# One order of 1,400 steps for another, with twelve zero products fewer: chunk-selected attention and a gated MLP on one core

## The chip, the core and the metric

The kernel runs on one core of a Trainium2 chip. The core has TensorE (PE in the profile; PEld is its loading of weights), VectorE (DVE), ScalarE (ACT), GpSimd (POOL) and SyncE (SP). The metric is device microseconds of one execution. The profile is of one execution, and its times count from the first instruction.

## The reference

Attention over chunks of 32 keys (batch 4, 8 heads, 768 positions, 64 dimensions): for each query an upper bound of its scores with every chunk is made from the chunk's minimum and maximum of k, the six best causal chunks are kept, and a softmax runs over them. A gated MLP with a product over positions follows.

```python
k_min = np.min(k_chunks, axis=3); k_max = np.max(k_chunks, axis=3)
ub = np.sum(np.maximum(q * k_min, q * k_max), axis=-1)      # each query with each chunk
top_chunks = np.argsort(np.where(causal, ub, -1e9), axis=-1)[..., -6:]
attn = softmax(where(selected & causal, q @ k.T / 8, -1e9)); x = attn @ v
h = np.maximum(x @ w_in, 0.0); u, v = h[..., :512], h[..., 512:]
v_n = (v - mean(v)) / sqrt(var(v) + 1e-6)
v_s = einsum('ts,bsd->btd', w_spatial, v_n) + b_spatial[:, None]
return (u * v_s) @ w_out
```

## The kernel before

The 32 heads are worked in 16 pairs (two heads share the 128 partitions), four pairs to a batch; i below is the pair, h the head in it. Loads fetch two pairs at once. Every step has a short name in a table `acts`, and a list written out in the program, ORDER, names all of them once. A loop at the end runs through it:

```python
with tc.manual_schedule():
    for name in ORDER.split():
        acts[name]()
```

An engine runs its own steps in the order of the list, one after the other; a step of one engine waits for those of others only through its data and its buffers. So the list fixes five queues at once: those of TensorE, VectorE, ScalarE, and the issues of loads on POOL's queue and of on-chip transfers and stores on SP's. The names:

- `dz`, `id0`, `id1`, `small`, `expand`, `mlat`, `mtri`: constants. `id1` (POOL, L538) finishes the identity matrix, which the transposes and `expand` (L565) need.
- `ring0` to `ring4` (L540 to L547): zero fills of the five q buffers, 0, 2 and 3 on VectorE, 1 on ScalarE, 4 on POOL.
- `khXh` (L589): copies `expand` into the half of the key operand that stays (X 0 to 3, reused by every fourth pair).
- `lk`, `lq`, `lv` (L604, L610, L615; the first ones L619), `win`, `wsp`, `wout`, `lb`: loads of keys, queries, values and weights, issued by POOL.
- `kT` (L680), `kTb` (L689): transposes of k on TensorE. `kc` copies the result out of PSUM from pair 8 on; `kmax`, `kmin` (L704) reduce it by chunks; `kb` (L731) sets up the bounds' operand; `kop` (L738, L740) puts k into the key operand, by copy up to pair 7 and by a transfer on SP after.
- `qT` (L745), `rq` (L754, L756), `ub` (L762, L765), `top` (L775), `sel` (L801): the bounds, the six best and the selection, written beside q.
- `aT` and `ac` (L820, L823): q with its selection, transposed on TensorE and copied; from pair 8 on `aTd` (L826) does it by one transposing transfer on SP. Pair 0 does it in parts: `selA0`, `aTA00`, `acA00` and so on.
- `scihg` (L833), `exihg` (L842), `tri` (L848), `av` (L859), `rc`, `nm` (L864, L869): scores in six tiles g, their exponentials, the causal triangle, the products with the values, and the division. The quotients go to one of two buffers x16.
- `x` puts x16 transposed into xT, by TensorE (`xp`, L884) and a copy in batch 0 and for pair 15, else by a transposing transfer on SP (L878).
- `vbt`, `ubt`, `sbt`, `obt` (L957), each in parts of two products: the MLP of batch b, tile t. `va`, `ua` (ScalarE), `bs`, `vs`, `vn`, `gt` (VectorE) stand between; `gd` transposes the gated tile on SP, `oc` (L1020) copies the output, `os` stores it.
- `dm` is 42 products of zeros at the start, and `dm0`, `dm1` and so on are one such product each (L895). They write a PSUM tile that nothing reads.

The MLP of a batch runs among the scores of the next one. PLAN holds the parameters: `dum` is the number of single zero products, and each name under `flip` runs on the other one of ScalarE and VectorE than it does by default (for `oc`, `ac` and `kh` the default is ScalarE, for `kc` and `kop` of pairs 2 to 7 VectorE).

Of the kernel before, what the change touches and what calls it, by code (L numbers as in the profile page):

```python
# [390 lines left out]
PLAN = {'late': 40, 'mlp_first': 8, 'qbuf': 5, 'kbuf': 6, 'vbuf': 6, 'dum': 64, 'warm0': 5.3, 'kcp': 8, 'flip': ['ac10', 'ac41', 'ac51', 'ac60', 'ac71', 'gd34', 'kc10', 'kc12', 'kc13', 'kc9', 'kh00', 'kh11', 'kop00', 'kop40', 'kop71', 'oc01', 'oc03', 'oc13', 'oc21'], 'gp': ((3, 4), (3, 5)), 'lm': 0.2, 'lm2': 1.2, 'tm': 0.8, 'dum0': 42, 'split': 1, 'rpool': (4,), 'ract': (1,)}  # L391

ORDER = """
dz id0 dm ring3 lk010 ring2 ring1 lk000 ring0 lq010 small id1 lq000 expand lk001 kh00 kh30 kh11 lk011 kT0 kh21 mlat
dm0 kTb0 lq011 kmin0 dm1 dm2 dm3 dm4 dm5 kop01 dm6 dm7 dm8 dm9 dm10 dm11 lq001 kmax0 qTb0 kh31 qT0 dm12 lk11 dm13 dm14
dm15 dm16 kb0 dm17 dm18 dm19 rq00 dm20 rq01 dm21 dm22 dm23 dm24 dm25 dm26 kop00 dm27 dm28 dm29 dm30 lk10 kh20 kT1 ub0
kmax1 kTb1 kh01 lv0 dm31 dm32 dm33 dm34 dm35 dm36 dm37 dm38 dm39 top00 dm40 dm41 kop11 dm42 qT1 kmin1 lq10 dm43 dm44
dm45 kop10 dm46 dm47 dm48 dm49 dm50 dm51 dm52 dm53 selA0 dm54 top01 kh10 mtri aTA00 dm55 kb1 dm56 dm57 dm58 sel0 rq11
lq11 aTB0 dm59 rq10 dm60 dm61 dm62 dm63 acA00 ub1 wsp0 acB0 sc000 top10 win00 sc001 ex000 aTA01 top11 sc002 lk20 ex001
acA01 sc005 kT2 sel1 ex002 sc004 kop20 lk21 ex005 sc013 ex004 sc011 kmin2 ex013 aT10 lq20 sc003 ex011 sc010 ac10 av000  # L400
ex003 kop21 aT11 lq21 ex010 sc015 av001 sc100 kmax2 ex015 av002 ac11 lv1 sc012 rc00 kb2 ex012 qT2 nm00 sc102 ex100
rq21 kT3 lk31 ex102 av010 rq20 sc014 kmax3 sc112 ex014 win21 ub2 sc101 ex112 kmin3 win11 sc104 qT3 ex101 sc111 top20
# [12 lines left out]
ex513 lq61 v01.0 bs02 av411 ex505 aT60 va04 bs00 v01.2 tri50 av412 ac60 sc514 va01 v03.0 lv3 rc41 vs02 nm41 sc603 ub7
ex603 bs01 v03.2 x4 sc511 ex514 lb top70 wsT0 ex511 av500 vs01 top71 sc512 lv4 va03 sc515 av501 sel7 wsT1 ex515 wsc0
sc600 ex512 av502 vs00 aT61 wsc1 ex600 v05.0 lq50 rc50 ac61 nm50 kT8 sc601 v05.2 kmax8 lq51 ex601 aT70 va05 sc604
kmin8 av510 lk61 ac70 sc613 sc602 u01.0 kc8 ex604 tri51 qT8 bs05 ex613 av511 wsT2 lk50 ex602 kb8 u01.2 rq80 sc611 rq81
u00.0 ex611 bs03 sc610 aT71 ua01 wsc2 av512 u00.2 ex610 vs05 bs04 sc704 wsT5 ua00 u02.0 vs04 ex704 ac71 wsT4 vs03 rc51
u02.2 rs0 nm51 sc605 sc614 wsc5 ub8 ex605 x5 ex614 sc612 wsc4 tri60 av600 ua02 sc700 vn00 av601 wsT3 ex612 vn04 sc701  # L420
ex700 u04.0 top80 av602 wsc3 sc703 u03.0 vn01 ex703 sc615 u04.2 rc60 ex701 nm60 u03.2 ua04 u05.0 top81 ua03 av610 sel8
sc702 vn03 ex615 sc710 aTd8 kT9 ex702 vn02 tri61 sc712 ex710 av611 kmin9 s00.0 lk60 ex712 u05.2 kop80 kmax9 av612
kop81 sc715 sc705 ua05 s00.2 wout1 rc61 ex715 qT9 vn05 kc9 sc711 s01.0 nm61 ex705 sc714 kop91 kb9 s00.4 rq91 tri70 x6
av700 rq90 s01.2 gt00 sc713 s02.0 ex713 gd00 av701 ub9 ex714 kT10 top90 s01.4 ex711 kop90 s02.2 top91 tri71 sc802 sel9
sc800 gt01 sc801 ex802 aTd9 av702 wout3 s02.4 ex801 rc70 wout2 s03.0 nm70 ex800 sc804 gt02 qT10 ex804 av710 kmax10
gd01 sc803 sc805 av711 sc810 ex803 s04.0 kmin10 ex805 av712 ex810 gd02 sc815 s03.2 tri80 ex815 rc71 sc812 kb10 kc10
nm71 s03.4 wout0 s04.2 ex812 x7 gt03 lv7 kT11 sc813 rq100 av800 ex813 sc811 rq101 gd03 av801 s05.0 kmax11 ex811 sc814
av802 s05.2 ex814 kop101 rc80 kmin11 s04.4 sc905 sc901 ub10 ex905 nm80 ex901 sc904 s05.4 kb11 gt04 ex904 sc900 av810
ex900 kc11 sc911 sc903 o01.0 ex911 top100 sc915 o00.0 top101 ex915 ex903 sc902 sel10 av811 o01.2 ex902 gt05 aTd10 qT11
sc910 oc01 tri90 v10.0 rq110 o00.2 tri81 kop100 rq111 sc914 v10.2 oc00 gd04 v11.0 lq60 ex914 ub11 ex910 av812 v11.2  # L430
gd05 lv5 va10 rc81 o02.0 nm81 va11 v13.0 top110 o02.2 kop110 top111 lq71 v14.0 sel11 oc02 sc912 bs10 av900 ex912 sc913
kT12 ex913 aTd11 v13.2 kmax12 v14.2 tri91 va13 av901 sc1000 kmin12 va14 sc1002 lk71 av902 ex1000 sc1012 v12.0 rc90
ex1002 nm90 o03.0 lk70 ex1012 bs11 sc1004 sc1005 av910 ex1004 bs14 qT12 av911 ex1005 o03.2 kc12 vs14 vs11 v12.2 oc03
sc1010 kop121 v15.0 va12 rq121 x8 av912 sc1003 sc1001 rc91 bs12 u10.0 ex1001 v15.2 rq120 os02 ex1010 u11.0 nm91 kop120
va15 u10.2 vs10 kop111 bs13 av1000 ua10 u11.2 os01 bs15 o04.0 ex1003 x9 kb12 kT13 ua11 vs13 tri100 o04.2 kmax13 sc1015
sc1014 oc04 sc1013 av1001 ub12 vs12 ex1014 kmin13 av1002 o05.0 ex1015 ex1013 sc1101 top120 u12.0 kc13 vs15 sc1011
rc100 top121 sc1104 ex1101 o05.2 kop130 sel12 ex1011 u13.0 nm100 os00 qT13 ex1104 kop131 tri101 u12.2 rq131 rs1 sc1100
aTd12 av1010 oc05 lv6 vn10 sc1103 sc1102 ua12 vn11 u13.2 ex1103 vn13 av1011 u14.0 ua13 vn14 u15.0 ex1100 rq130 av1012
u14.2 kb13 ex1102 rc101 vn15 u15.2 ua14 vn12 s10.0 ua15 sc1114 ub13 s10.2 top130 sc1110 sc1105 s10.4 nm101 ex1105
ex1110 s11.0 tri110 gt10 kT14 ex1114 s11.2 kmin14 lq70 gd10 s12.0 av1100 kmax14 sc1115 s11.4 ex1115 s12.2 gt11 sc1113  # L440
av1101 s12.4 kc14 gd11 sc1112 s14.0 gt12 ex1112 sc1111 av1102 top131 ex1113 s13.0 gd12 rc110 sel13 ex1111 s15.0 nm110
s14.2 tri111 sc1203 aTd13 sc1200 s14.4 ex1203 av1110 ex1200 gt14 s13.2 x10 av1111 sc1213 av1112 sc1201 ex1213 kT15
rc111 nm111 sc1202 s13.4 kmax15 ex1202 x11 sc1205 s15.2 ex1201 qT14 gt13 s15.4 ex1205 sc1215 kc15 sc1204 o10.0 ex1204
rq140 sc1210 kop151 av1200 gt15 ex1215 o10.2 os05 tri120 av1201 kb14 os03 rq141 sc1212 oc10 sc1302 kmin15 o12.0 gd13
ex1210 av1202 ex1212 ub14 rc120 sc1300 nm120 o12.2 gd15 ex1300 top140 sc1214 v21.0 ex1302 top141 v20.0 oc12 sel14
sc1310 ex1214 v21.2 sc1211 ex1310 qT15 sc1313 aTd14 ex1211 sc1303 rq150 v20.2 va21 rq151 tri121 av1210 ex1313 kb15
o11.0 gd14 ex1303 ub15 v23.0 va20 top150 av1211 sc1314 kop150 top151 sc1311 av1212 ex1314 bs20 o11.2 kop140 ex1311
# [21 lines left out]
def kernel(  # L469
# [622 lines left out]
```

## Time and profile before

| | us |
|---|---|
| median of 13 runs (201.11 to 204.09) | 202.28 |
| the profiled execution | 202.13 |
| its span, first to last instruction | 200.4 |
| TensorE busy | 191.6 |
| VectorE busy | 156.4 |
| ScalarE busy | 149.1 |
| POOL busy | 80.8 |

In groups of instructions each line has the source line, the engine and operation, what is written and read, the shapes and the count, then busy time and the mean length. In stretches of time a line gives the stretch, its length, then busy us of PE, PEld, DVE, ACT and POOL with counts, the granted TensorE clock, the busy share of the DMA queues and GB/s. In order of time a line gives start, us, engine, line and operation; in brackets stands how long the engine had been idle and what ended that. SPq is the issue of a transfer on SP. A line of DMA issues ends with the time from issue to landing. Matmuls overlap in TensorE, so that the distance between two starts, not a length, tells its rate.

### The profile page before, as it was taken

The numbers are of one execution on the slowest core, as the hardware profiler recorded it, in microseconds if no ns is written. First come the engines' busy times: TensorE is split into PE (matmuls) and PEld (weight loads), VectorE is DVE, ScalarE is ACT, GpSimd is POOL, SyncE is SP. The second block draws the span as 40 slices with busy tenths as digits, with TensorE's granted clock in tenths as the row PEclk, the third lists the DMA queues.
The fourth block names the chain that finished last, engine by engine and source line by source line (L and its number), as shares of the span: only waits on it lengthen the run. The fifth ranks groups of instructions, "written<-read, shape, count | busy, mean of one in ns | idle before, by whom it ended". The sixth has DMA issues, their size and how long they took to land.

```text
span 200.4 us, 5309 instructions
## 1 busy us (share of the span) xinstructions
PE 191.6 (96%) x2057; PEld 121.7 (61%) x2057; DVE 156.4 (78%) x475; ACT 149.1 (74%) x296; POOL 80.8 (40%) x97
## 2 busy tenths in 40 slices
PE   7989999999999999999999899999999999999992
PEld 7876778776676755565565455656555555444451
DVE  6899899999999999898798689797378337257430
ACT  5879899999989985777889873689899751664151
POOL 7999956462998143434731422011212130000000
PEclk9999999999999999999999999999999999999999
DMA  6999999999899999999999999788774265342335
GB/s 40 97 127 166 163 162 181 172 193 106 57 143 120 154 115 191 138 191 148 161 139 152 236 196 165 145 216 108 220 116 43 79 121 149 114 179 85 79 127 213
DMA packets 114761, 28.60 MB, mean 143 GB/s; under 512 B 108720, under 2 KB 111280, under 8 KB 114736
## 3 DMA queue, kind: packets, MB, share of 16 engines
q0 software_dynamic: 76544, 12.20, 88.2%
q1 hardware_dynamic: 38192, 16.06, 40.6%
q8 instruction: 16, 0.26, 0.6%
q14 instruction: 9, 0.07, 0.1%
HBM read 24.38 MB, written 6.29 MB: 153 GB/s over the span
## 4 chain that ended last, share of the span: by engine, by line
PE 67%; DMA 11%; DVE 9%; POOL 6%; ACT 2%; issue 2%; SPq 0%; POOLq 0%; DVEq 0%; ACTq 0%
PE mlp L957 39%; PE sc L833 12%; PE acc L859 8%; DMA xT<-x 5%; DMA qs<-in_q_dram 3%; DMA kh<-kT 2%; DVE kmm L704 2%; POOL k L619 2%; PE trq L745 2%; PE tra L820 1%; POOL qs L619 1%; DVE max L775 1%; DVE x L869 1%; PE ub L765 1%; PE kTp L680 1%
## 5 line engine op out<-in xcount | busy, mean ns | idle before, releaser
L842 ACT ACTIVATE e<-sc 128x512 f16<-128x512 f32 (+1 forms) x192 | 93.9, 564 | 19.3 <-PE sc L833 16.6
L833 PE MATMUL sc<-a,kh 128*128 128x512 f16 (+3 forms) x256 | 61.2, 305 | 0.7 <-DMA kh<-kT 0.4
L957 PE MATMUL mlp<-w_in_sb,xT 128*128 128x512 f16 x192 | 52.2, 379 | 0.0
L848 POOL TENSOR_SCALAR_AFFINE_SELECT e<-e 128x768 f16<-128x768 f16 x24 | 21.0, 877 | 75.6 <-ACT e L842 64.3
L859 PEld LDWEIGHTS <-e 128*128 128x128 f16 x672 | 31.3, 97 | 15.5 <-DVE x L869 1.7
L957 PE MATMUL mlp<-vn,wsT 128*128 128x512 f16 x144 | 38.8, 379 | 0.0
L859 PE MATMUL acc<-vt,e 128*128 128x65 f16 x672 | 35.8, 193 | 0.8 <-DVE x L869 0.7
L704 DVE TENSOR_REDUCE kmm<-kTp 128x24 f16<-128x768 f16 x32 | 29.6, 947 | 1.8 <-PE kTp L680 1.8
L833 PEld LDWEIGHTS <-kh 128*128 128x128 f16 x256 | 22.6, 97 | 13.4 <-DMA kh<-kT 0.9
L957 PE MATMUL mlp<-w_out_sb,gT 128*128 128x512 f16 x92 | 26.1, 379 | 0.0
L957 PEld LDWEIGHTS <-xT 128*128 128x128 f16 x192 | 17.1, 98 | 14.3 <-DMA xT<-x 0.2
L1000 DVE SCALAR_TENSOR_TENSOR g<-mlp,b_col,u 128x512 f16<-128x512 f32 x24 | 17.8, 746 | 9.0 <-PE mlp L957 6.9
L1020 ACT COPY o<-mlp 128x512 f32<-128x512 f32 x19 | 11.1, 589 | 16.9 <-PE mlp L957 16.5
L979 DVE BATCH_NORM_STATS2 stats<-vraw 128x6 f32<-128x512 f32 x24 | 15.9, 677 | 5.8 <-ACT vraw L974 5.8
L869 DVE TENSOR_TENSOR x<-acc,rec 128x384 f16<-128x384 f32 x32 | 17.6, 551 | 2.4 <-DMA xT<-x 1.9
L957 PEld LDWEIGHTS <-wsT 128*128 128x128 f16 x144 | 12.6, 97 | 10.1
L989 ACT ACTIVATE u<-mlp 128x512 f16<-128x512 f32 x24 | 14.0, 597 | 5.0 <-PE mlp L957 4.1
L775 DVE MAX8 max<-ub 128x8 f32<-128x8 f32 (+4 forms) x160 | 15.2, 163 | 1.7 <-PE ub L765 1.6
L974 ACT ACTIVATE vraw<-mlp 128x512 f32<-128x512 f32 x24 | 14.2, 608 | 2.4 <-PE mlp L957 2.4
L610 POOL DMA_DIRECT2D qs<-in_q_dram x14 | 14.5, 1045 | 1.6 <-DMA w_in_sb<-in_moe_w_in_dram 0.8
L604 POOL DMA_DIRECT2D k<-in_k_dram x14 | 14.8, 1062 | 0.4 <-DMA ws_raw<-in_moe_w_spatial_dram 0.4
L864 DVE RECIPROCAL rec<-acc 128x6 f32<-128x6 f32 x32 | 5.9, 185 | 9.7 <-PE acc L859 9.6
(85 smaller groups left out, 243.3 us busy)
## 6 DMA issues: line engine op xcount, KB each, us to landing
out_dram<-o SPq DMA_DIRECT2D x23, 256.0 KB, 2.3
vt<-in_v_dram POOLq DMA_DIRECT2D x8, 384.0 KB, 9.2
k<-in_k_dram POOLq DMA_DIRECT2D x14, 192.0 KB, 7.1
qs<-in_q_dram POOLq DMA_DIRECT2D x14, 192.0 KB, 7.0
kh<-kT SPq DMA_DIRECT2D x16, 96.0 KB, 4.9
ws_raw<-in_moe_w_spatial_dram POOLq DMA_DIRECT2D x6, 192.0 KB, 6.7
w_in_sb<-in_moe_w_in_dram POOLq DMA_DIRECT2D x8, 128.0 KB, 8.3
w_out_sb<-in_moe_w_out_dram POOLq DMA_DIRECT2D x4, 128.0 KB, 5.3
```

The lines of the kernel that those rows point to most:

```text
L604: nc.gpsimd.dma_start(out=k_tile(g)[:, :, :, hi, :].rearrange("p x t d -> p (x t) d"), in_=source(k, b, 2 * hp + 2 * hi, 2))
L610: nc.gpsimd.dma_start(out=t.rearrange("p x t d -> p (x t) d"), in_=source(q, b, 2 * hp + 2 * hi, 2))
L704: nc.vector.tensor_reduce(self.kmm[:, m, :], src, axis=AX.X, op=op, negate=(m == 1))
L775: nc.vector.max(self.max8[:, qi - 1, hi, :], self.ub[:, c0:c0 + CPT * (qi + 1)])
L833: mm(sc[:, col:col + n], lhsT=self.kh[hi][:, t * P:(t + 1) * P], rhs=self.a[:, q0 // P:(q0 + n) // P, hi, :], start=True, stop=not diag)
L842: nc.scalar.activation(out=self.e[hi][:, g * 512:g * 512 + width], in_=self.sc[hi, g][:, 0:width], func=Act.Exp, scale=scale)
L848: nc.gpsimd.affine_select(out=blk, in_=blk, compare_op=Alu.is_ge, fill=0.0, base=0, channel_multiplier=-1, pattern=[[0, NQT], [1, P]])
L859: mm(self.av[hi][:, qi, :], lhsT=self.e[hi][:, c:c + P], rhs=self.v[hi][:, t, 0:D + 1], start=first and n == 0, stop=last and n == len(blo ...
L869: nc.vector.tensor_tensor(self.x16[:, :, hi, :], in0=self.av[hi][:, :, 0:D], in1=self.rec[hi].to_broadcast([P, NQT, D]), op=Alu.mult)
L957: mm(st[kind, ti], lhsT=lhsT, rhs=rhs, start=(j == 0), stop=(j == n - 1))
L979: nc.vector.bn_stats(st["stats", ti], st["vraw"][:, ti, :])
L1000: nc.vector.scalar_tensor_tensor(g, in0=st["s", ti], scalar=b_col[:, ti:ti + 1], in1=st["u"][:, ti, :], op0=Alu.add, op1=Alu.mult)
```

## The change

The code of every step stays. PLAN and ORDER change. Single zero products go from 64 to 52. The zero fills stay on their engines (`rpool` and `ract` are as they were), but stand elsewhere in the list: `ring1` now comes after `rq01` on ScalarE, and `id1` comes after four load issues on POOL, not three. The flips put `kh00`, `kh21`, `kh30`, `kh31` on VectorE (before `kh00`, `kh11`), `ac11`, `ac40`, `ac41`, `ac51`, `ac70`, `ac71` on VectorE (before `ac10`, `ac41`, `ac51`, `ac60`, `ac71`), `kop31`, `kop40`, `kop51`, `kop71` on ScalarE (before `kop40`, `kop71`), eight `oc` on VectorE (before four), `kc8` to `kc11` on ScalarE (before 9, 10, 12, 13), and `gd34` on VectorE (before ScalarE). All five queues are in another order nearly throughout; the diff is cut to PLAN, the head, the start of the first MLP and the part around pairs 8 to 11.

```diff
-PLAN = {'late': 40, 'mlp_first': 8, 'qbuf': 5, 'kbuf': 6, 'vbuf': 6, 'dum': 64, 'warm0': 5.3, 'kcp': 8, 'flip': ['ac10', 'ac41', 'ac51', 'ac60', 'ac71', 'gd34', 'kc10', 'kc12', 'kc13', 'kc9', 'kh00', 'kh11', 'kop00', 'kop40', 'kop71', 'oc01', 'oc03', 'oc13', 'oc21'], 'gp': ((3, 4), (3, 5)), 'lm': 0.2, 'lm2': 1.2, 'tm': 0.8, 'dum0': 42, 'split': 1, 'rpool': (4,), 'ract': (1,)}
+PLAN = {'late': 40, 'mlp_first': 8, 'qbuf': 5, 'kbuf': 6, 'vbuf': 6, 'dum': 52, 'warm0': 5.3, 'kcp': 8, 'flip': ['ac11', 'ac40', 'ac41', 'ac51', 'ac70', 'ac71', 'kc10', 'kc11', 'kc8', 'kc9', 'kh00', 'kh21', 'kh30', 'kh31', 'kop00', 'kop31', 'kop40', 'kop51', 'kop71', 'oc01', 'oc03', 'oc05', 'oc11', 'oc12', 'oc13', 'oc23', 'oc25'], 'gp': ((3, 4), (3, 5)), 'lm': 0.2, 'lm2': 1.2, 'tm': 0.8, 'dum0': 42, 'split': 1, 'rpool': (4,), 'ract': (1,)}
 
 ORDER = """
-dz id0 dm ring3 lk010 ring2 ring1 lk000 ring0 lq010 small id1 lq000 expand lk001 kh00 kh30 kh11 lk011 kT0 kh21 mlat
-dm0 kTb0 lq011 kmin0 dm1 dm2 dm3 dm4 dm5 kop01 dm6 dm7 dm8 dm9 dm10 dm11 lq001 kmax0 qTb0 kh31 qT0 dm12 lk11 dm13 dm14
-dm15 dm16 kb0 dm17 dm18 dm19 rq00 dm20 rq01 dm21 dm22 dm23 dm24 dm25 dm26 kop00 dm27 dm28 dm29 dm30 lk10 kh20 kT1 ub0
-kmax1 kTb1 kh01 lv0 dm31 dm32 dm33 dm34 dm35 dm36 dm37 dm38 dm39 top00 dm40 dm41 kop11 dm42 qT1 kmin1 lq10 dm43 dm44
-dm45 kop10 dm46 dm47 dm48 dm49 dm50 dm51 dm52 dm53 selA0 dm54 top01 kh10 mtri aTA00 dm55 kb1 dm56 dm57 dm58 sel0 rq11
...
-sc410 kop71 x3 sc500 av401 ac51 v00.0 ex410 kmin7 av402 ex502 v00.2 tri41 ub6 ex500 kop70 sc504 sc503 lq41 sc505 top60
...
-ex900 kc11 sc911 sc903 o01.0 ex911 top100 sc915 o00.0 top101 ex915 ex903 sc902 sel10 av811 o01.2 ex902 gt05 aTd10 qT11
-sc910 oc01 tri90 v10.0 rq110 o00.2 tri81 kop100 rq111 sc914 v10.2 oc00 gd04 v11.0 lq60 ex914 ub11 ex910 av812 v11.2
-gd05 lv5 va10 rc81 o02.0 nm81 va11 v13.0 top110 o02.2 kop110 top111 lq71 v14.0 sel11 oc02 sc912 bs10 av900 ex912 sc913
-kT12 ex913 aTd11 v13.2 kmax12 v14.2 tri91 va13 av901 sc1000 kmin12 va14 sc1002 lk71 av902 ex1000 sc1012 v12.0 rc90
-ex1002 nm90 o03.0 lk70 ex1012 bs11 sc1004 sc1005 av910 ex1004 bs14 qT12 av911 ex1005 o03.2 kc12 vs14 vs11 v12.2 oc03
-sc1010 kop121 v15.0 va12 rq121 x8 av912 sc1003 sc1001 rc91 bs12 u10.0 ex1001 v15.2 rq120 os02 ex1010 u11.0 nm91 kop120
...
-sc1014 oc04 sc1013 av1001 ub12 vs12 ex1014 kmin13 av1002 o05.0 ex1015 ex1013 sc1101 top120 u12.0 kc13 vs15 sc1011
-rc100 top121 sc1104 ex1101 o05.2 kop130 sel12 ex1011 u13.0 nm100 os00 qT13 ex1104 kop131 tri101 u12.2 rq131 rs1 sc1100
-aTd12 av1010 oc05 lv6 vn10 sc1103 sc1102 ua12 vn11 u13.2 ex1103 vn13 av1011 u14.0 ua13 vn14 u15.0 ex1100 rq130 av1012
...
+dz id0 dm small lk010 ring0 lk000 ring3 lq000 ring2 lq010 id1 lk011 expand lk001 kh00 kT0 kh11 kh31 lq011 kh30 dm0
+kTb0 kmin0 dm1 dm2 dm3 dm4 dm5 kop01 dm6 lq001 dm7 dm8 dm9 dm10 dm11 kmax0 qTb0 mlat qT0 rq01 dm12 lk11 dm13 dm14 dm15
+dm16 rq00 dm17 dm18 dm19 dm20 dm21 dm22 dm23 kb0 ring1 kop00 ub0 lk10 dm24 dm25 top00 kTb1 kT1 top01 lv0 kop10 dm26
+dm27 dm28 selA0 dm29 kmin1 aTA00 aTA01 kh10 dm30 dm31 dm32 dm33 dm34 mtri dm35 kmax1 dm36 dm37 dm38 dm39 dm40 dm41
+kh01 dm42 dm43 dm44 dm45 dm46 dm47 lq10 sel0 qT1 acA00 kop11 dm48 kb1 aTB0 rq10 lq11 sc000 kh20 rq11 dm49 dm50 dm51
+acB0 ub1 win10 acA01 ex000 sc005 sc001 kh21 win01 ex005 top10 sc002 ex001 kT2 win21 top11 ex002 sc004 lb sc013 kmax2
+ex004 sc010 ex013 lk21 sc003 sel1 av000 kop21 ex010 sc015 aT10 ex003 lq21 kop20 aT11 ex015 sc011 ac10 av001 kmin2
+sc012 lk20 av002 ex011 sc102 rc00 ac11 ex012 sc100 kb2 ex102 nm00 qT2 wout1 qT3 ex100 rq21 sc014 lq20 sc112 rq20 ex014
...
+ex411 sc414 rq60 ex501 sc502 rq61 xp3 ex414 kmax7 sc413 ex502 av400 lk41 aT51 x2 ex413 sc500 sc410 ac51 kop71 lq40
+sc504 av401 x3 ub6 ex500 av402 kop70 v00.0 ex410 lq41 sc503 kmin7 v00.2 ex504 sc510 ex503 sc512 top60 lv3 v02.0 ex510
...
+lv7 s05.2 ex812 x7 kmax11 av801 s04.0 sc810 s05.4 rq101 ex810 kop100 sc901 kmin11 ub10 kop101 ex901 sc903 sc813 top100
+gd03 av802 ex903 o00.0 rc80 ex813 top101 sc814 s04.2 nm80 ex814 o00.2 kb11 sel10 sc911 tri81 kop111 gt05 sc904 sc914
+ex911 s04.4 aTd10 lq60 oc00 av810 gt04 sc900 ex904 av811 o01.0 ex914 lq70 sc913 ex900 qT11 o01.2 ex913 lq71 av812
+sc902 oc01 v10.0 ex902 v11.0 rc81 lv5 gd04 nm81 sc910 sc915 rq110 v10.2 ex915 rq111 sc905 o02.0 kop110 va10 lk71 v11.2
+gd05 ub11 va11 av900 lv6 top110 v13.0 ex905 o02.2 bs11 av901 v13.2 bs10 oc02 lk70 v14.0 top111 va13 kT12 vs10 sel11
+ex910 v14.2 tri90 kmin12 v12.0 va14 sc912 sc1002 kc12 v12.2 ex912 aTd11 vs11 sc1003 kmax12 av902 va12 tri91 sc1000
+o03.0 ex1002 rc90 bs14 qT12 x8 ex1000 v15.0 nm90 ex1003 o03.2 bs13 sc1010 av910 ex1010 sc1012 rq121 sc1004 rq120 u10.0
...
+oc04 sc1104 tri100 o05.0 ex1104 kc13 av1001 u12.0 ex1014 vs12 vs14 av1002 sel12 sc1011 sc1101 rc100 kmax13 sc1114
...
+sc1110 vn10 u15.2 ex1112 vn12 sc1105 u14.2 vn15 u13.0 ua14 rq131 sc1100 av1010 rq130 ua15 u13.2 vn13 ex1105 s10.0
...
 """
```

## The prediction

> **What bounds the kernel now.** I read the stages first, then who waits for whom, then the order of time at the two places where TensorE stands still. The page gives the engines' totals, and the stretches give them by stage (busy us of PE, PEld, DVE, ACT, POOL).
>
> ```profile
> span 200.4 us, 5309 instructions
> PE 191.6 (96%) x2057; PEld 121.7 (61%) x2057; DVE 156.4 (78%) x475; ACT 149.1 (74%) x296; POOL 80.8 (40%) x97
> ...
> 6.64:48.86 42.22, 39.62 (x627) 31.74 (x626) 40.89 (x136) 39.04 (x77) 31.24 (x40) 1.00 1.90 154
> 49.40:72.00 22.60, 22.60 (x287) 15.42 (x284) 22.05 (x78) 20.35 (x43) 15.12 (x15) 1.00 2.20 125
> 72.00:95.00 23.00, 22.56 (x246) 13.64 (x245) 20.95 (x59) 16.61 (x36) 10.22 (x13) 1.00 1.39 155
> 95.00:118.00 23.00, 22.23 (x235) 13.09 (x234) 18.29 (x60) 19.66 (x40) 8.99 (x9) 1.00 1.66 179
> 140.00:166.00 26.00, 26.00 (x238) 14.68 (x237) 14.16 (x33) 20.19 (x44) 5.32 (x6) 1.00 0.56 116
> ```
>
> Busy TensorE is not TensorE at its rate, so I used the distance from one matmul's start to the next: 0.216 us for 512 columns, 0.109 for 256, 0.056 for 128, 0.030 for the 65 of the value products, 0.025 for the 48 of the bounds. Summed over all real products this is 176.9 us. Of it only 32.7 us are done when the first MLP product v00.0 starts at 49.4 us: 16.7 us are lost in the head. The other 144.2 us take until 196.2 us, a loss of 2.6 us; 4.2 us of copy and store follow. So there are two bounds: up to 49 us VectorE (40.9 of 42.2 us busy) with ScalarE close behind, then TensorE, where only a late operand costs anything. The chain of waits shows such operands, all DMA landings:
>
> ```profile
> 75.40 5.00 DMA kh<-kT
> 80.45 0.82 PE sc L833 x3
> ...
> 103.85 9.26 DMA xT<-x
> 113.14 0.57 DVE x L869
> 113.75 0.45 PE acc L859 x9
> ```
>
> By the distances of starts TensorE loses 0.22 us at 76.87, 0.56 at 80.45, 0.23 at 110.02 and 0.87 at 113.75: 1.88 us.
>
> **The change, part by part.** *Zero products, 64 to 52.* They stand where TensorE waits for VectorE or a load, so twelve fewer shorten nothing by themselves: 0 us. Their other use is the clock. The 42 products of dm load their weights in 4.39 us (104 ns each), the 19 after 8 us in 1.10 us (58 ns); the granted clock is full from 6.7 us on and no gap of TensorE there exceeds 0.91 us. In the new order I find gaps up to about 1.5 us (waiting for kb0 near 9 us, for rq11 near 15 us). The Trainium skill, "TensorE: Matmul & The Clock Gate", speaks against the change here: about 3.4 us of idleness halve the clock (Part 1), and transposes don't count as busy (Part 4), and most head products are transposes. By the rule one window of 3.4 us at half speed could cost at most half of it, 1.7 us; by the row, where stretches of transposes went by at full clock, 0. I take 0, with 1.7 as upper end.
>
> *Head, VectorE.* These rows set its start:
>
> ```profile
> 3.08 0.85 POOL L619 DMA_DIRECT2D qs<-in_q_dram  x1
> 3.99 0.33 POOL L538 TENSOR_SCALAR_AFFINE_SELECT identity<-identity 128x128 f16<-128x128 f16 x1
> 4.35 0.55 DVE L565 TENSOR_SCALAR expand<-identity 64x768 f16<-64x768 f16 x1 [0.17 <-POOL identity L538]
> 4.96 1.36 DVE L589 COPY kh<-expand 64x768 f16<-64x768 f16 x2
> 6.64 1.82 DVE L704 TENSOR_REDUCE kmm<-kTp 128x24 f16<-128x768 f16 x2 [0.32 <-PE kTp L680]
> ```
>
> id1 is moved on POOL's queue behind a fourth load issue (lq010 as well as lq000): +0.85 us, and expand, which needs it, starts at 5.20. Between expand and the first kmm there are now three kh copies, not two: 1.36/2 = 0.68 more. From expand to the end of two copies took 1.97 us, so kmm starts at 5.20 + 1.97 + 0.68 = 7.85 instead of 6.64: 1.2 us late. kh21 adds a fourth copy (0.68) near 17 us. Against that, two VectorE idles go, 0.24 us (before pair 1's kmm, now behind pair 0's selection) and 0.52 (for the q of pair 2, landing at 20.27 as before): 1.2 + 0.68 - 0.76 = 1.1. The flips up to x3 cancel: kop31 and kop51 leave (2 x 0.555), ac40 and ac51 come (2 x 0.54). x3, the last copy before the first MLP, moves from 48.9 to 50.0. But 0.67 us more of TensorE's work (sc504, ub6, av402) now stands ahead of v00.0, so the TensorE-bound stretch loses 1.1 - 0.67 = 0.43.
>
> *Head, ScalarE.* ring1 (1.47 us) ran at 2.10, under the wait for expand; now it stands behind rq01, and kop10, kh10, kh01, kop11, kh20 follow it before the first exp. kop10 also needs kTb1, which TensorE now runs behind ub0 (about 10.4, so kTb1 is done near 11.5). Five copies of 0.81 bring the first exp to 15.6 instead of 14.81. ScalarE was idle for 1.1 us between there and 48.6, which takes up most of that and of the flips (two kop at 0.79 more, one ac at 0.85 less). It stays within VectorE's lag. For the head as a whole I take +0.5 us; the ends are -0.5 (both engines closer packed) and +3 (VectorE's two removed idles come back elsewhere and ScalarE's lag adds).
>
> *Copies of o.* Four more go to VectorE (0.688 each), off ScalarE (0.589), all after 84 us, where VectorE has 2 to 5 us free in each stretch above: 0. Without that room one costs 0.7 where its buffer is waited for.
>
> *The four stalls.* I measured leads: TensorE work, by the distances above, that the order puts between an issue and its first user. kop80 had 5.3 us and landed after 5.0; it now has 6.9. x8, whose landing frees the x16 buffer for pair 10, had 8.7 us to av1010 and took 9.26; it now has 13.1. The w and q loads that ran beside aTd8 come earlier. If nothing replaces them the four stalls return 1.88 us.
>
> *Loads and SP, near 90 to 115 us.* This decides. Before, POOL issued here lq60, lv5, lq71, lk71, lk70 (1152 KB in 94.55 to 102.2) and SP's transposing loads went out among them:
>
> ```profile
> 94.55 1.04 POOL L610 DMA_DIRECT2D qs<-in_q_dram  x1
> 95.58 1.44 POOL L615 DMA_DIRECT2D vt<-in_v_dram  x1
> 96.99 1.04 POOL L610 DMA_DIRECT2D qs<-in_q_dram  x1
> ...
> 100.11 2.05 POOL L604 DMA_DIRECT2D k<-in_k_dram  x2
> ...
> 98.68 3.67 SPq L826 DMA_TRANSPOSE a<-qs  x1
> ...
> a<-qs SPq DMA_TRANSPOSE x1, 11.2
> ...
> a<-qs SPq DMA_TRANSPOSE x1, 3.7
> ```
>
> The first a row is aTd11's issue, the second its time to landing, the third that of aTd13 at 125.9, when POOL had nothing in flight. aTd11 had a lead of 11.0 us and TensorE waited 0.23 us. In the new order lq70 and lv6 join the same bunch: seven issues in one piece between tri81 and tri90 (5 x 1.04 + 2 x 1.44 = 8.1 us of POOL), 1728 KB. aTd10 is issued at the first of them with a lead of 8.8 us (before 7.1; it took 5.3 in a lull), aTd11 has 8.1 to its first user sc1104, queued behind kop111, aTd10, gd04, kop110 and gd05. Behind sc1104 all of TensorE's queue stands. Bounds: aTd10 between 5.3 (lull) and 11.2 (crowd), a stall of 0 to 2.4; aTd11 between 3.7 and 11.2 x 1728/1152 = 16.8, a stall of 0 to 8.7. The two don't add up, since a stall at the first gives the second time to land. The nearest row is aTd11's own 11.2 in the lighter crowd: 3.1 at least; I take 3.5 for both.
>
> Here the rule differs from the row. "DMA: Bandwidth & Descriptors" (Queues, rings and completion order) has each DMA engine alternate between the queues with work, whatever their backlog. Two queues, equal shares: 2 x 3.7 = 7.4 us, less than 8.1, no stall. The row says 11.2 with two queues, issue time on SP included, and I follow it. lq60 (lead 10.5 for 5.9 taken), lv5 (14.0 for 9.4) and lk70 (18.1 for 15.2) still fit, narrowly. After 118 us all leads exceed the landings before (aTd13 6.0 for 3.7, gd12 4.3 for 3.2): 0.
>
> **Sum.** 200.4 + 0.5 - 1.9 + 3.5 = 202.5 us of span. The profiled execution took 202.13 us, 1.73 outside its span, and lies 0.15 under the median: 202.5 + 1.9 = **204.4 us**, 1.0% slower.
>
> **Rivals.** *The leads hold (other side).* If aTd10 lands within 8.8 us and aTd11 within 8.1, the 1.9 us return and nothing replaces them: 200.4 + 0.5 - 1.9 + 1.9 = 200.9 us. For it: seven of the eight a transfers of before landed in under 7.7 us. Against: the only one in a comparable crowd took 11.2. *The crowd scales.* The 16.8 us for aTd11 happen, 8.7 of stall instead of 3.5: 209.6; and values between. For it: DMA engines read 9 of 10 up to 125 us. Against: some bunched loads are only moved from later. *The head slips.* Its upper end, +3, without the DMA stall: 200.4 + 3 - 1.9 + 1.9 = 203.4; with half of it 205. *Nothing happens.* Searched orders trade one small stall for another: 202.3; for it, most of the work is the same products at the same rate in either order.
>
> **How the numbers follow.** Late a transfers 0.46; crowd scaling 0.14; leads hold 0.20; head slips 0.10; nothing 0.10. The first runs from 203.0 to 206.0, with a twentieth of the whole below 203.3. 0.5% of the median is 1.0 us, about what these runs can tell from none. Faster (under 201.3): most of leads-hold, 0.17. Same: the rest of it, nothing, and the lower edges of the slow cases, 0.16. Slower: 0.67. The range, 200.6 to 208.6, leaves out the best of leads-hold and the worst of crowd scaling.
>
> **What would show it.** Right: first kmm near 7.9 us, first exp near 15.6, v00.0 near 50; no wait at kop80's and x8's users; TensorE idle for some us before scores of pair 10 or 11, released by DMA a, with landings over 9 us. Wrong: those landings under 8 us; v00.0 before 49; a granted clock below 1 in the head; a new wait past 118 us.

## The result and the profile after

The changed kernel takes 205.05 us in the median (204.4 to 209.21, 11 runs), the kernel before beside it 202.66 (201.08 to 205.01, 48 runs): a ratio of 1.013, with a 95% interval of 1.0099 to 1.016. The change makes the kernel slower by about 1.3%; the forecast was 204.4 us, 1.05% slower. The profiled execution took 209.27 us, 207.6 of it span, and is one of the longest: of the 14 executions on record with their granted clock the seven at 0.996 and more took 204.4 to 205.1 us, the four at 0.988 to 0.992 took 205.8 to 206.6, and the three at 0.98, the profiled one among them, 208.6 to 209.3. Ratios, here and below, are of fast executions alone (within 1.5% of the fastest of their kernel; in e2 two of six), medians and ranges are not.

The page of the kernel after, its head and the rows of slices (each digit a fortieth of the span, tenths of busy time or of the full clock):

```profile
span 207.6 us, 5289 instructions
...
PE 192.8 (93%) x2045; PEld 121.9 (59%) x2045; DVE 159.3 (77%) x481; ACT 145.3 (70%) x290; POOL 81.0 (39%) x97
...
PE   7789989999999999999459999999999999999992
...
PEclk9999999999999999999958999999999999999998
```

TensorE has two slices at 4 and 5 tenths where everything around is at 9, and in the second of them the clock is at 5. A slice is 5.2 us, so this lies between 98.6 and 109 us. The stretches of the kernel after, with the same columns as before (length, then busy us of PE, PEld, DVE, ACT, POOL, the clock, the DMA share, GB/s):

```profile
6.64:48.86 42.22, 38.43 (x603) 30.61 (x601) 41.34 (x137) 40.12 (x78) 34.97 (x45) 1.00 1.93 160
49.40:72.00 22.60, 22.20 (x283) 15.25 (x282) 21.81 (x77) 20.09 (x42) 11.67 (x12) 1.00 1.81 114
72.00:95.00 23.00, 22.61 (x253) 14.01 (x251) 20.21 (x57) 17.90 (x37) 11.48 (x14) 1.00 1.37 155
95.00:118.00 23.00, 18.03 (x163) 10.19 (x162) 13.88 (x48) 12.25 (x26) 7.20 (x7) 0.85 1.91 151
140.00:166.00 26.00, 26.00 (x250) 14.91 (x249) 17.04 (x57) 22.02 (x48) 4.32 (x5) 1.00 0.77 164
```

The other four stretches have TensorE about as busy as before. In 95 to 118 us TensorE was idle for 5.0 us, and its records show 163 matmuls instead of 235; the DMA share rose from 1.66 to 1.91. The chain of waits of the kernel after names what ended the wait:

```profile
92.89 0.43 PE mlp L957 x2
93.33 0.06 PE sc L833
93.39 12.56 DMA a<-qs
105.95 0.04 issue
105.99 0.59 PE sc L833
106.58 0.85 PE mlp L957 x2
107.43 0.43 PE sc L833 x2
```

This is aTd10, issued at 93.39 and landed after 12.56 us; sc1002 is the first user, and all of TensorE's queue stood behind it for 5.14 us, by the distances of starts. Then comes a second loss that the chain doesn't call a wait: two MLP products of 512 columns take 0.85 us, where before and elsewhere they take 0.43. From 103.9 to 110.7 us the granted clock was one half:

```profile
103.90:110.70 6.80, 4.71 (x22) 2.32 (x22) 2.47 (x6) 2.17 (x4) 0.00 (x0) 0.50 1.64 116
```

What was around it, from the order of time of the kernel after (POOL's load issues and SP's transposing ones) and from its DMA issues between 90 and 118 us:

```profile
91.86 3.06 POOL L610 DMA_DIRECT2D qs<-in_q_dram  x3
...
93.39 2.97 SPq L826 DMA_TRANSPOSE a<-qs  x1
94.90 1.44 POOL L615 DMA_DIRECT2D vt<-in_v_dram  x1
96.29 1.05 POOL L604 DMA_DIRECT2D k<-in_k_dram  x1
97.29 1.46 POOL L615 DMA_DIRECT2D vt<-in_v_dram  x1
98.69 1.07 POOL L604 DMA_DIRECT2D k<-in_k_dram  x1
...
101.05 7.79 SPq L826 DMA_TRANSPOSE a<-qs  x1
```

```profile
vt<-in_v_dram POOLq DMA_DIRECT2D x2, 384.0 KB, 18.5
...
k<-in_k_dram POOLq DMA_DIRECT2D x2, 192.0 KB, 19.3
...
a<-qs SPq DMA_TRANSPOSE x2, 13.2
```

The seven issues of the forecast stand there in one piece, and aTd10 is issued between them. Before, a k load of this stretch landed after 15.2 us; here two take 19.3 in the median. The second row of aTd's is aTd11; it took 13.80 us and yet made TensorE wait for nothing: the wait for aTd10 had moved its user back as well.

The start of the kernel after, in order of time, for the steps of the head:

```profile
4.79 0.34 POOL L538 TENSOR_SCALAR_AFFINE_SELECT identity<-identity 128x128 f16<-128x128 f16 x1
...
5.17 0.55 DVE L565 TENSOR_SCALAR expand<-identity 64x768 f16<-64x768 f16 x1 [0.98 <-POOL identity L538]
...
5.78 1.73 DVE L589 COPY kh<-expand 64x768 f16<-64x768 f16 x3
...
7.43 1.81 DVE L704 TENSOR_REDUCE kmm<-kTp 128x24 f16<-128x768 f16 x2
```

The three copies of kh take 1.73 us together, and the first kmm starts at 7.43, not 6.64.

### The profile page after: what moved, and what is told of

Read it like the earlier page. It is cut to its first block, busy times and chain, and to the rows that moved or that the text cites. A ratio compares the mean times of both kernels' runs of the same rounds, so it can differ in the third digit from the quotient of the medians.

```text
span 207.6 us, 5289 instructions
## 1 busy us (share of the span) xinstructions
PE 192.8 (93%) x2045; PEld 121.9 (59%) x2045; DVE 159.3 (77%) x481; ACT 145.3 (70%) x290; POOL 81.0 (39%) x97
## 4 chain that ended last, share of the span: by engine, by line
PE 62%; DVE 18%; DMA 9%; POOL 6%; ACT 2%; issue 1%; POOLq 0%; DVEq 0%
PE mlp L957 40%; PE sc L833 10%; PE acc L859 7%; DMA a<-qs 6%; DVE kmm L704 4%; DMA qs<-in_q_dram 3%; DVE x L869 2%; DVE vn L994 2%; DVE max L775 2%; POOL qs L619 2%; POOL k L619 2%; PE trq L745 1%; DVE rq L756 1%; ACT e L842 1%; DVE rq L754 1%
## 5 line engine op out<-in xcount | busy, mean ns | idle before, releaser
L833 PE MATMUL sc<-a,kh 128*128 128x512 f16 (+3 forms) x256 | 62.6, 308 | 6.3 <-DMA a<-qs 5.0
L859 PEld LDWEIGHTS <-e 128*128 128x128 f16 x672 | 31.9, 98 | 14.2 <-DVE x L869 1.0
L859 PE MATMUL acc<-vt,e 128*128 128x65 f16 x672 | 36.4, 194 | 0.5 <-DVE x L869 0.4
L957 PE MATMUL mlp<-w_out_sb,gT 128*128 128x512 f16 x92 | 27.0, 385 | 0.1
L1020 ACT COPY o<-mlp 128x512 f32<-128x512 f32 x15 | 8.9, 591 | 11.6 <-PE mlp L957 11.5
L775 DVE MAX8 max<-ub 128x8 f32<-128x8 f32 (+4 forms) x160 | 15.2, 162 | 1.9 <-PE ub L765 1.8
```

What stands on the lines that cost most here:

```text
L775: nc.vector.max(self.max8[:, qi - 1, hi, :], self.ub[:, c0:c0 + CPT * (qi + 1)])
L833: mm(sc[:, col:col + n], lhsT=self.kh[hi][:, t * P:(t + 1) * P], rhs=self.a[:, q0 // P:(q0 + n) // P, hi, :], start=True, stop=not diag)
L859: mm(self.av[hi][:, qi, :], lhsT=self.e[hi][:, c:c + P], rhs=self.v[hi][:, t, 0:D + 1], start=first and n == 0, stop=last and n == len(blo ...
L957: mm(st[kind, ti], lhsT=lhsT, rhs=rhs, start=(j == 0), stop=(j == n - 1))
```

## The experiments

Theories: *crowd* says that the loss is the transposing transfers aTd10 and aTd11, late because seven loads are issued in one piece around them. *SP's queue* says that they are late behind other transfers of SP itself; e1, e4 and e9 move loads and leave SP's order as it was. *Head* says that the new start costs it (VectorE and ScalarE late). *Clock* says that TensorE's lower clock, in the head for want of zero products or behind the wait, carries part of it. Ratios are to the kernel before on the same chip, whose medians in these comparisons lay between 203.3 and 203.8 us.

| kernel | median us (range, runs) | ratio, 95% |
|---|---|---|
| e0, after itself | 206.47 (204.39 to 209.49, 6) | 1.0141 [1.0054, 1.0227] |
| e1, after, two loads later | 205.43 (203.94 to 206.37, 6) | 1.0115 [1.0051, 1.018] |
| e2, before, two loads earlier | 211.36 (207.91 to 211.57, 6) | 1.0263 [1.0155, 1.0372] |
| e3, after with the head of before | 206.88 (205.88 to 207.73, 6) | 1.0191 [1.0129, 1.0252] |
| e4, after, bunch dissolved | 205.32 (203.79 to 207.1, 10) | 1.0084 [1.0049, 1.0119] |
| e5, before with the head of after | 202.74 (201.74 to 203.49, 22) | 0.9965 [0.9944, 0.9986] |
| e6, e4 with two head steps earlier | 204.52 (203.04 to 208.4, 22) | 1.0076 [1.005, 1.0103] |
| e7, after without single zero products | 206.96 (205.82 to 209.32, 6) | 1.0149 [1.0099, 1.0199] |
| e8, after, zero products in the wait | 205.97 (205.2 to 209.22, 6) | 1.0126 [1.008, 1.0172] |
| e9, after, loads elsewhere, head as e6 | 203.22 (202.54 to 207.34, 22) | 1.000 [0.9977, 1.0024] |
| e10, e5 with two head steps earlier | 202.45 (200.93 to 204.0, 22) | 0.9962 [0.9934, 0.999] |
| e11, before itself | 203.32 (201.31 to 209.16, 22) | 0.9991 [0.9959, 1.0022] |

### e0: the changed kernel once more

No edit.

> The changed kernel itself, for a profile of a usual execution beside the others. Crowd theory (seven loads in one piece make the selection transfer of pair 10 late): 1.3% slower than the kernel before, the transfer lands over 9 us after its issue and TensorE stands 2 to 5 us before the scores of pair 10. Head theory (the later start of VectorE and ScalarE is what costs): the stall is small and the first MLP product is more than 2 us later than before.

Measured: 206.47 us, 1.0141. Its profiled execution (209.49 us) repeats the other almost to the step: aTd10 issued at 93.49, 12.86 us to its landing, TensorE stands 5.31 us ahead of sc1002, half clock from 103.93 to 110.76. So the wait comes again with the order. But this execution, too, is the longest of its six: both profiles of the changed kernel show the long kind. The link of clock and time is looser here: two executions with a clock of 0.992 took 207.25 and 208.38 us.

### e1: two of the seven loads later

```diff
-ex911 ... ex914 lq70 sc913 ...
-... va11 av900 lv6 top110 ...
+... sc1104 tri100 lq70 o05.0 ex1104 ...
+... ex1101 tri101 lv6 vs15 sc1102 ...
```

> The changed kernel with two of the seven loads, lq70 and lv6, put back behind tri100 and tri101; all else stays. Crowd theory: the transfer of pair 10 lands within 9 us, its stall falls below 1 us, that of pair 11 may keep up to 2 us: 1.5 to 3 us faster than the changed kernel. Head theory, and the theory that SP's own queue is too full: no change, within 0.5 us of the changed kernel.

Measured: 205.43 us; the profiled execution 204.65, all of it at full clock. The order of time of TensorE in e1, at the two first users:

```profile
102.06 0.38 PE L833 MATMUL sc<-a,kh 128*128 128x512 f16 x1 [1.09 <-DMA a<-qs]
...
112.36 0.38 PE L833 MATMUL sc<-a,kh 128*128 128x256 f16 x2 [1.27 <-DMA a<-qs]
```

With five loads in the bunch aTd10 lands after 8.95 us and aTd11 after 11.23; by the distances of starts the waits are 1.26 and 1.43 us instead of 5.14 and none. In the profiles the loss behind v00.0 halves, from 9.30 us in e0 to 4.57. In the times the gain over e0 is small (1.0115 against 1.0141, intervals overlapping): the median falls by 1.0 us, where 1.5 to 3 were expected. The place of two loads changes the waits, but with five the two transfers still land later than the leads allow.

### e2: the same two loads earlier in the kernel before

```diff
-v11.0 lq60 ex914 ...
+v11.0 lq60 lq70 ex914 ...
-sc1002 lk71 av902 ...
+sc1002 lk71 lv6 av902 ...
-... av1010 oc05 lv6 vn10 ...
-... kmin14 lq70 gd10 ...
+... av1010 oc05 vn10 ...
+... kmin14 gd10 ...
```

> The kernel before with lq70 moved behind lq60 and lv6 behind lk71, so that the same seven loads are in flight together; all else stays. Crowd theory: the transfer of pair 11 (11.2 us in the kernel before) takes 13 us or more and its scores wait 2 to 5 us: 2 to 5 us slower than the kernel before. Head theory and the theory of SP's queue: no change, within 0.5 us.

Measured: 211.36 us, 1.0263, the largest loss of all and larger than that of the whole change. Four of its six executions took 211.3 to 211.6 us. But the place differs from the expected one. The chain of waits of e2:

```profile
95.80 1.99 POOL qs L610 x2
97.80 13.57 DMA vt<-in_v_dram
111.36 0.14 issue
111.50 0.45 PE acc L859 x9
```

The value load lv5, issued behind lq60 and lq70, landed 13.57 us later, and av1000 waited 3.04 us for it. aTd11 took 12.18 us, less than the 13 expected, and its scores didn't wait; the kernel before reached 12.35 with five loads (e11). So moving two loads costs time without anything else of the change, but here a load came late behind other loads, not a transposing transfer. The half clock came here too, 3.41 us of it (111.79 to 115.20) behind a wait of 3.04.

### e3: the head of before in the changed kernel

```diff
-'dum': 52, 'flip': [..., 'kh00', 'kh21', 'kh30', 'kh31', 'kop00', 'kop31', ...]
+'dum': 64, 'flip': ['ac10', ..., 'kh00', 'kh11', 'kop00', ...]
-dz id0 dm small lk010 ring0 ... (after's list up to v00.0)
+dz id0 dm ring3 lk010 ring2 ... (before's list up to v00.0, for the same steps)
```

> The changed kernel with the order and the engines of the kernel before up to the first MLP product, the same steps as in its own head. Crowd theory: the first MLP product comes 0.5 to 1 us earlier and the total falls by just that, to about 0.9% over the kernel before; the stall before the scores of pair 10 stays. Head theory: the total falls by 2 us or more, to the kernel before.

Measured: 206.88 us, 1.0191. It is no faster than the changed kernel, and the gain that the head theory asks for isn't there. It says little of the head, though: v00.0 comes at 51.09 us, not earlier than the changed kernel's 50.67, so the old head's steps brought nothing forward in this order. The head is judged by e5. In its profiled execution (206.97 us) aTd10 takes 9.20 us and aTd11 12.11, with waits of 1.44 and 2.19 us, without any step of the new head.

### e4: the bunch dissolved

```diff
-... lq70 ... lq71 ... lk71 ... lv6 ... lk70 ... (between tri81 and tri90)
+av601 tri60 lq70 lq71 lk71 lk70 sc702 ...
+ex1101 tri101 lv6 vs15 ...
```

> The changed kernel with lq70, lq71, lk71 and lk70 moved forward behind tri60, where no load is in flight, and lv6 back behind tri101; of the seven loads only lq60 and lv5 stay. Crowd theory: both selection transfers land within 8 us, both stalls go (2.7 us in the profile with two loads moved), and the total falls to within 0.7% of the kernel before on either side. Theory of SP's own queue, whose order is untouched: stalls of over 1 us stay.

Measured: 205.32 us, 1.0084. aTd11 lands after 6.65 us and nobody waits for it; aTd10 still takes 9.45, and at sc1002 0.89 us are left. But the four loads now run beside the key operand of pair 8. The chain of e4:

```profile
75.98 7.60 DMA kh<-kT
83.58 0.05 issue
83.63 0.39 PE sc L833 x2
```

This wait, 1.63 us at sc803, is a new one: kop80 took 7.60 us where the changed kernel had 5.77. The loads were moved off one transfer with a short lead and onto another. This wait stands against what was won at pairs 10 and 11; only about a third of the loss came back.

### e6: e4 with two steps of the head earlier

```diff
-... lk000 ring3 lq000 ring2 lq010 id1 lk011 expand ...
+... lk000 id1 ring3 lq000 ring2 lq010 lk011 expand ...
-kh00 kT0 kh11 kh31 ...   dm23 kb0 ring1 kop00 ub0
+kh00 kT0 ring1 kh11 kh31 ...   dm23 kb0 kop00 ub0
```

> The same, and in the head id1 moved forward behind two load issues on POOL and ring1 to the front of ScalarE's queue. By my working of the head expand starts 0.9 us earlier, the first reduction 0.6 to 0.9 us earlier, the first exponential 0.5 to 1.5 us earlier, and the total falls by 0.5 to 1 us against the run without it, below the kernel before. If other waits of the head take its place, no change.

Measured: 204.52 us, 1.0076. The first kmm is at 6.85 and the first exponential at 14.51 (e4 as after: 7.43 and 15.11), and v00.0 starts at 50.01 instead of 51.09. The median falls by 0.8 us, the ratio by only 0.0008, well within the intervals. The 1.37 us at sc803 stay.

### e9: the loads at a place with room

The trace of the changed kernel shows POOL's load queue empty between the landing of lk60 at 67.3 us and the next load issue at 74.4. So four of the loads go behind lk60, and lv6 as in e1; the head is that of e6.

```diff
-kT8 lk60 aT70 ...
+kT8 lk60 lk71 lk70 lq70 lq71 aT70 ...
-... lq70 ... lq71 ... lk71 ... lv6 ... lk70 ... (between tri81 and tri90)
+ex1101 tri101 lv6 vs15 ...
```

> The changed kernel with id1 and ring1 moved as there, lv6 behind tri101, and lq70, lq71, lk71, lk70 behind lk60, so that they have landed when the selection transfer of pair 8 is issued. Crowd theory: no wait of over 0.5 us before the scores of pairs 8, 10 and 11, 1 to 1.5 us faster than with the four loads behind tri60 (ratio 1.0076): 0.999 to 1.003. If it is the number of bytes before 118 us rather than their crowding: still 1.007.

Measured: 203.22 us, 1.000 [0.9977, 1.0024]. The whole 1.3% is gone, with the same steps on the same engines, the same bytes and everything else of the new order behind the head in place. Against e6 (1.0076), which has the same head, only the place of four loads differs. The place isn't quite free: in the profile TensorE waits 0.80 us at 66.10 for a triangle of POOL that stands behind the load issues. Its profiled execution is its longest one (207.34 us): there aTd10 took 10.58 us with only lq60 and lv5 of the seven loads around it, TensorE stood 2.89 us and the clock was half for 3.41 us. So the lead at sc1002 remains short, and sometimes it still doesn't suffice. Of the 22 executions 21 took 202.5 to 204.4 us; none of these was profiled, so that the gain is shown by the times, and the waits that went by no trace.

### e5: the head of after in the kernel before

```diff
-'dum': 64, (head flips of before)
+'dum': 52, (head flips of after)
-dz id0 dm ring3 lk010 ring2 ... (before's list up to v00.0)
+dz id0 dm small lk010 ring0 ... (after's list up to v00.0, for the same steps)
```

> The kernel before with the order and the engines of the changed kernel up to the first MLP product, the same steps as in its own head. By my working x3 and the first MLP product come 1.1 us later and the total rises by 0.5 to 1.1 us. Head theory: it rises by 2 us or more. If both heads are equal: within 0.3 us.

Measured: 202.74 us, 0.9965 [0.9944, 0.9986]. The new head with 52 zero products, alone, makes the kernel no slower, by the times even 0.35% faster. Its stretches:

```profile
6.64:49.40 42.76, 39.01 (x608) 30.96 (x606) 41.92 (x138) 40.48 (x78) 31.39 (x40) 1.00 1.88 154
49.40:95.00 45.60, 45.38 (x531) 29.18 (x530) 43.79 (x136) 36.94 (x76) 24.93 (x28) 1.00 1.76 139
```

v00.0 is at 49.76, though the head steps stand where they stand in the changed kernel (first kmm 7.43, first exponential 15.10, first copy of x into xT 49.16 against 49.14). It starts before x3's copy on VectorE (50.09 us), so it doesn't need it. In the changed kernel sc504, ub6 and av402 stand ahead of v00.0 in TensorE's queue, and ub6 itself starts 0.29 us late by the distances, so that v00.0 comes at 50.67.

### e10: e5 with the two head steps of e6

Edit as in e6, on e5.

> The kernel before with the changed kernel's head, and in it id1 behind two load issues and ring1 first on ScalarE. With the head alone the ratio was 0.9965; the two moves brought the first exponential forward by 0.6 us and the first MLP product by 1.1 in the other run. Expected: first MLP product 0.5 to 1 us earlier, ratio 0.991 to 0.996, faster than both kernels. If the middle absorbs it: 0.9965 as before.

Measured: 202.45 us, 0.9962 [0.9934, 0.999]; with e5 the fastest of all, and faster than both kernels. The two moves added nothing to e5. The first exponential comes at 14.51 us, 0.6 earlier, and then TensorE's row in e10 is

```profile
18.50 0.43 PE L859 MATMUL acc<-vt,e 128*128 128x65 f16 x9 [1.18 <-DMA vt<-in_v_dram]
```

The first value load lands when it lands, so the lead won was spent waiting for it, and v00.0 is at 50.21, no earlier than e5's 49.76.

### e7: no single zero products

```diff
-'dum': 52
+'dum': 0
```

and `dm0` to `dm51` leave the list; the 42 of `dm` stay. They are all that is left out.

> The changed kernel without any of the 52 single zero products; the 42 of the start stay. By my working they shorten nothing and only hold the clock: with gaps of up to 3 us in the head the clock may fall to half for a time, and since VectorE sets the pace there, 0 to 1 us slower than the changed kernel (ratio 1.013 to 1.02). If the clock stays full: the same as the changed kernel within 0.3%.

Measured: 206.96 us, 1.0149. The stretches of e7 in the head:

```profile
4.90:10.60 5.70, 2.20 (x35) 1.80 (x36) 5.33 (x13) 3.69 (x4) 5.62 (x9) 1.00 1.63 104
10.58:17.41 6.83, 5.67 (x50) 4.54 (x51) 6.11 (x31) 5.29 (x8) 6.75 (x10) 0.50 1.90 123
```

The same stretches of the changed kernel have 4.15 us of busy TensorE in the first, and a clock of 1.00 in both. In all six executions of e7 the mean clock is 0.963 to 0.983. So the single zero products do hold the clock up in the head, and 52 of them were enough in the changed kernel's profiles. The loss of clock made v00.0 late (51.58 against 50.67), yet the times hardly show it (1.0149 against 1.0141 and 1.013): in the profiled execution the wait at sc1002 was 1.63 us instead of 5.14, with one of 1.97 us for lv5 at 113.96. That the later head shifted what follows against the loads is a guess.

### e8: zero products in the wait

```diff
-... va14 sc912 sc1002 kc12 ...
+... va14 sc912 dw sc1002 kc12 ...
+    def hold():
+        idle = ps_sc.tile([P, 512], F32, tag="sc", name="hold")
+        for _ in range(60):
+            mm(idle[:, 0:P], lhsT=idle_op, rhs=idle_op, start=True, stop=True)
```

> The changed kernel with 60 zero products (3.4 us at full clock) placed right before the scores of pair 10 that wait; their result is not read. If a wait[...] halves TensorE's clock and that is part of the loss: the clock stays full through that place, the profiled execution falls by about 2 us, the longest executions likewise, and the shortest rise by at most 1 us. If the clock is no part of it: no change or slower by up to 3 us.

Measured: 205.97 us, 1.0126. TensorE's row and the stretch that was at half clock in the changed kernel:

```profile
100.97 3.51 PE L902 MATMUL hold<-idle_op 128*128 128x128 f16 x60
104.31 0.38 PE L833 MATMUL sc<-a,kh 128*128 128x512 f16 x1
```

```profile
103.90:110.70 6.80, 6.80 (x74) 4.16 (x72) 4.02 (x11) 4.85 (x10) 0.00 (x0) 1.00 1.81 156
```

The clock stays full, and this execution took 205.32 us. It doesn't weigh the clock: aTd10 landed at 102.07 here, after 9.65 us and not 12.56, so that without the 60 products TensorE would have waited 1.1 us, too little to halve the clock by the other traces (2.19 us in e3 did not). The products (3.34 us) held TensorE 2.2 us longer than the transfer would have, and one of the six executions is still at 209.22 us with a clock of 0.988. Five of the six have a clock of 0.997 and more; of the 20 executions of the changed kernel in its own comparison and in e0, ten have 0.996 and more. The median falls by 0.5 us against e0, well inside the intervals.

### e11: the kernel before once more

No edit.

> The kernel before itself, for its profile and its spread beside the others. Ratio 1.000, within 0.3%; first MLP product near 49.4 us. If the head of the changed kernel costs nothing, its first MLP product comes as late as in the kernel before with that other head (49.8 us).

Measured: 203.32 us, 0.9991. Its profiled execution (203.86 us, v00.0 at 49.37) loses 4.52 us behind v00.0, that shown before the prediction (202.13 us) 2.77: waits of 1.07 us for aTd9, 0.89 for lv5 and 0.74 for x8, all landings between 88 and 116 us. aTd11 took 12.35 us here, 11.2 in the first profile. The kernel before lives at the edge of the same crowd; one execution of it is no measure to better than 2 us.

## Why the prediction came right, point by point

*The bounds.* TensorE's real products sum up to about 177 us in both kernels, and nothing was gained or lost in their rate at full clock. What differs is waits: behind v00.0 the profiled execution loses 9.31 us, that of before 2.77.

*Zero products, 0 us.* Right for 52: the clock is full from 4.9 to 103.9 us. The rule, with its estimate of at most 1.7 us, stood near: e7 shows half clock for 6.83 us once the single ones are gone, with TensorE busy, in part with transposes, for 5.67 us of it. The row answered for this change; what the rule warns of comes somewhere between 52 and none.

*Head, +0.5 us.* The steps came close: expand at 5.17 (5.20 forecast), first kmm 7.43 (7.85), first exponential 15.11 (15.6), x3 at 50.07 (50.0). The copies of kh were cheaper, three in 1.73 us instead of 2.04. Lost time of TensorE up to v00.0: 50.67 less the 32.7 of before and the 0.67 put ahead is 17.30, against 16.7: +0.6. So the size held in this order, but not the path: v00.0 doesn't wait for x3 (e5), and about half of the lag (0.29 us) is a wait of ub6 ahead of it. As a cause of the 1.3% it fell: e5 has the same early steps, v00.0 only 0.34 us late and no loss in its time.

*Four stalls, -1.9 us.* They went: kop80 took 5.77 us with no wait at sc803, and av1010 didn't wait for x8. Two new ones came behind v00.0, 0.43 us at 69.68 and 0.56 at 78.66, so 0.9 remains of the 1.9. *After 118 us, 0*: right, 0.24 us at 137.90 is all.

*Loads and SP, +3.5 us.* That the place of the loads costs the time is shown by runs: e9 removes the loss by moving five loads (and two steps of the head, which gave 0.1% or nothing in e6), and four loads alone are the difference between it and e6. SP's order is the same in e1, e4 and e9, so *SP's queue* alone doesn't explain the loss. In e2 two moved loads make a loss, though through a late load. The place was right (scores of pair 10), and that the two stalls don't add up as well.

The upper bound for aTd10 was wrong twice. Its landing of 11.2 us was taken from aTd11 in the lighter crowd and not scaled, though it was for aTd11; 12.56 and 12.86 came. And its lead of 8.8 us, counted as work in the order, was too long: from its issue at 93.39 to the end of the product ahead of sc1002 at 100.85 only 7.5 us passed, and 12.56 less 7.5 is the wait. (Of kop80 before the same count gave 5.3 us, more than its landing of 5.0, although it was waited for.) aTd11's 13.80 lies inside its 3.7 to 16.8. But the scaling with bytes isn't borne out. aTd11 took 6.20 to 6.65 us with two of the seven loads left in this stretch (e4, e6, e9), 10.7 to 12.35 with five (before, e11, e5, e10, e1) and 10.3 to 13.8 with seven; aTd10 took 7.97 to 10.58 with two, 8.95 with five (e1) and 9.2 to 12.86 with seven. More loads go with later landings, but the ranges overlap.

In place of 3.5 the profiled execution shows 5.14 of wait, and about 2.3 of half clock (half of the 4.7 us that TensorE worked at it) that no term of the sum had. In the usual execution it is less. An estimate: 205.05 less 1.7 around the span is 203.3; less 50.67 to v00.0, 143.5 of products and 4.2 of tail leaves 4.9 lost, of which the profile's small losses (9.31 - 5.14 - 2.3) take 1.9, so about 3.0 for the waits at pairs 10 and 11. That is near the 3.5. It is inferred from the median itself, since no profile of this kernel caught such an execution; e3, which has the same seven loads and full clock, shows 1.44 + 2.19 = 3.6 us of wait at the two users.

*The rule against the row.* The Trainium skill, "DMA: Bandwidth & Descriptors" (Queues, rings and completion order), lets each DMA engine take turns, packet by packet, between the queues that have work; equal shares and 7.4 us without a stall were the forecast's estimate from it. In the five traces that have all seven loads in one piece (after, e0, e3, e7, e8) aTd10 took 12.56, 12.86, 9.2, 9.3 and 9.65 us, all above 7.4. Alone such a transfer took 3.7 before and 3.83 here (aTd12). The packets of the changed kernel's trace show both sides. From 111 to 112 us, POOL's queue moved 415 and SP's 416: even turns. From 100 to 104 us, with aTd10 still under way, POOL's moved 2825 and SP's 365. So the estimate failed and the turns themselves need not have; what kept SP's packets back isn't shown, and transfers ahead in SP's own queue were left out of the 7.4.

*Sum.* 200.4 + 0.6 - 0.9 + 3.0 = 203.1 of span, and 204.8 with what lies around it. As the 3.0 was worked back from the median, that this closes proves nothing. The forecast's 204.4 came from a return that was too large by 1.0 and, by this estimate, a stall too large by 0.5, against a median of before, 202.28 us, that lay 0.4 us under that of all its runs. The mechanism was foreseen; that the number came within 0.7 us is in part luck, since a lead, a landing and a return were each wrong by a microsecond or more and no term held the half clock.

*Rivals.* The leads don't hold, the crowd doesn't scale to 8.7 us of stall, and "nothing happens" is out by the interval. *The head slips* is out by e5.

*Open.* How much the half clock adds in the long executions: they have the lower clock, but e8 doesn't settle it. Why e5 gains 0.35%, and whether e9, which has nearly the same head and not the gain, still loses as much elsewhere (the two intervals overlap): e5's profile has v00.0 0.34 us later than before and waits of 0.87, 0.60 and 0.48 us like before's; where the gain arises wasn't found. Why one execution has the transfer at 9 us and another at 13.

## What to carry to other kernels

A load that nobody waits for can still set the time: count, for each short-lead transfer, how many loads are issued around it, and move the loads to a stretch where the load queue is empty, not merely to an earlier one (e9 against e6). Take the landing time of a crowd from rows in a crowd, from several executions; the row from a lull (3.7 us) was wrong by a factor of three, and scaling by bytes (16.8 us) by more than the spread. Take a lead from the time of the issue in a trace, not from the place in the order. An order that is tight at one place moves its stall when something else moves by a microsecond, so judge it by many executions and not by one trace.

## What was not expected of the hardware

- TensorE's clock was halved in mid-kernel after a single wait: 6.83 us of half clock around and behind a wait of 5.14 us, 3.41 us behind waits of 3.04 (e2) and 2.89 us (e9); 2.19 us (e3) did not halve it. In the changed kernel it begins 3.05 us after TensorE went idle (100.85 to 103.9) and lasts 4.7 us past the end of the wait; in e2 it begins at 111.79, when the wait is already over (111.50). The stretches of one clock in these traces, 3.41, 6.83, 98.99 and 105.81 us, are 1, 2, 29 and 31 times 3.413 us. A wait of three microseconds thus can cost more than its length.
- The issue of a transposing transfer on SP itself can be long in the crowd: SP's row for aTd11 is 7.79 us in the changed kernel and 6.52 in e3, but 3.47 in e2 with seven loads too; with five it is 4.14 in e1, 3.67 and 4.95 in the two profiles of before. aTd12 in the changed kernel has 1.81.
- A copy of kh (64x768) took 0.35 us at the shortest on VectorE in the changed kernel and 0.78 at the longest; the two of before took 0.57 and 0.77. The cause wasn't tried.
- The head's lead can be worth nothing: in e10 0.6 us of it was absorbed by the wait for the first value load.
